# Holding seven V heads on chip instead of four, with FFN weights in four column blocks, in a decode attention layer with its backward pass

## The chip, the cores and the metric

One core of one Trainium2 chip. Times are device microseconds of a whole execution; a trace covers one profiled execution and its span is about 2 us shorter than the time. The kernel before was run again beside each experiment, on the same chip: its single runs lie between 814.0 and 827.2 us over all chips, so each experiment is compared with the runs of before that it shared. The changed kernel was not run again beside the experiments: where a text below says "less than the changed kernel", the two medians come from different rounds, and as the medians of before differ by up to 3.7 us between rounds, such a difference is good to some 4 us.

Ratios are computed as the mean time of one kernel's runs over the mean of the other's in the same rounds, so they are not quite the ratios of the medians quoted.

## The reference

One token goes through a pre-layernorm attention block and a bilinear FFN block; the outputs are the result and the gradients of all inputs.

```python
# x: 1 x 448; 16 query heads, 8 KV heads of 256; caches 8 x 32768 x 256, the window is the last W = 4096 rows
q = layernorm(x) @ wq
p = softmax(q @ K[window].T / 16);  o = p @ V[window]
h  = x + o @ wo
h2 = h + (g * u) @ w_down        # g = layernorm(h) @ w_gate, u = layernorm(h) @ w_up, F = 1792
# returned: h2, dx, dK_cache, dV_cache, dwq, dwo, dw_gate, dw_up, dw_down
```

What matters here: dK_cache and dV_cache have the shape of the caches, 134 MB each. Outside the window they are zero, so 235 MB of zeros must be stored. Inside the window each KV head needs its K and V in a forward pass (pass 1), and its V once more in the backward pass (pass 2), which writes 2 MB of dV and 2 MB of dK per head.

## The kernel before

GpSimd issues 103 zero stores of 2 MB from one zero buffer. They wait for nothing but room in their queue. SP issues everything else.

```python
zeros = ar(0, ZW)                       # ZW = 8192 elements, 16 KB per partition
for g in range(G):
    for o in (out_2, out_3):            # dK, dV
        if g == G - 1 and o is out_3:
            continue
        reg = zero_rows(o, g, 0, 5 if g == G - 1 else NZ, ZW)
        for i in range(reg.shape[0]):
            ZQ.dma_start(out=reg[i], in_=zeros)          # ZQ = nc.gpsimd
```

Pass 1 has three K slots and four V slots (HELD = 4). V of the heads 0 to 3 is overwritten by V of the heads 4 to 7; those four stay for pass 2, which starts with them and loads the others again.

```python
for g in range(G):
    p_f = p_next
    if g + 1 < G:
        p_next = scores(g + 1)          # transposes of K, q.K, softmax
    moments(g, p_f)                     # M = V.T (p*K), and p.V, p.K
    if g + 3 < G:
        load_kv(K_slot[g % 3], A_k_cache, g + 3)
    if g + HELD < G:
        load_kv(V_slot[g % HELD], A_v_cache, g + HELD)
    if g == G - 2:
        LD.dma_start(out=wo_sb, ...)    # LD = nc.sync (SP)
# ... the whole of w_gate and w_up, in rows of 10752 bytes per partition; w_down was loaded in pass 1
```

In the middle stand the out projection, the FFN forward and backward, and the gradient of o. Pass 2:

```python
stage = [...] * 3                        # three buffers of 2 MB for dV and dK
order = list(range(HELD, G)) + list(range(HELD))
for it, g in enumerate(order):
    ... dots(V_sb, ...)                  # transposes of V, do.V
    stV, stK = stage[stc % 3], stage[(stc + 1) % 3]
    stc += 2
    for l in range(8):                   # 16 rank-4 products, copied from PSUM into stV and stK
        ...
    for o_ap, st_ in ((out_3, stV), (out_2, stK)):
        LD.dma_start(out=o_ap[0, g, Sk - W:, :]..., in_=st_)
    for job in plan[it]:                 # weight gradients: outer products, stored from two buffers
        job()
    if it == 6:
        nc.vector.memset(ar(VB, ZW), 0.0)          # a slot that is free by now
for o, g, n0, n1, f in late_jobs:        # the last nine 2 MB pieces of zeros, 18.9 MB, as four stores of 4 MB and one of 2 MB
    ... LD.dma_start(out=reg[i], in_=ar(VB + ZW - f, f))
```

The late zero stores read a slot that is cleared only near the end, so they cannot be issued earlier.

Of the kernel before, what the change touches and what calls it, by code (L numbers as in the profile page):

```python
# [21 lines left out]
NB = 7  # L22
# [5 lines left out]
HELD = 4  # L28
# [4 lines left out]
def kernel(  # L33
# [13 lines left out]
    VB = 16 * KB  # L47
    MB = VB + HELD * 16 * KB
    RB = MB + 32 * KB
    TOTAL = RB + 81 * KB + 128  # L50
    arena = const.tile([128, TOTAL], bf16)

    def ar(off, n):
        return arena[:, off:off + n]

    zeros = ar(0, ZW)
    V_slot = [ar(VB + 16 * KB * i, T * Dh).rearrange("p (t d) -> p t d", d=Dh) for i in range(HELD)]
    M_sb = [ar(MB + 4 * KB * g, 4 * KB).bitcast(f32).rearrange("p (v h d) -> p v h d", v=2, h=2) for g in range(G)]
    wqA = ar(MB, 24 * KB).rearrange("p (c j) -> p c j", c=3)
    wqB = ar(MB + 24 * KB, 4 * KB)  # L60
    K_slot = [ar(RB + o * KB, T * Dh).rearrange("p (t d) -> p t d", d=Dh) for o in (16, 32, 0)]
    KT_slot = [ar(RB + (48 + 2 * i) * KB, 2 * KB).rearrange("p (e t k) -> p e t k", t=4, e=2) for i in range(3)]
    pK_slot = [ar(RB + (54 + 4 * i) * KB, 4 * KB).rearrange("p (t h d) -> p t h d", t=4, h=2) for i in range(2)]
    wo_sb = ar(RB, 28 * KB).rearrange("p (j n) -> p j n", n=D)
    wg_sb = [ar(RB + 28 * KB + 6272 * i, 3 * F).rearrange("p (c f) -> p c f", c=3) for i in range(2)]
    wgB_sb = [ar(RB + 28 * KB + 6272 * i + 3 * F, FH) for i in range(2)]
    junk = ar(RB + 105 * KB // 2, F)
    o_rows = junk[0:H, 0:2 * Dh].bitcast(f32)
    om = junk[:, 2 * Dh:4 * Dh].bitcast(f32).rearrange("p (a j) -> p a j", a=8)
    h_row = ar(RB + 119 * KB // 2, 2 * D)[0:1].bitcast(f32)  # L70
    diag = ar(RB + 56 * KB, F)
    wd_sb = ar(RB + 62 * KB, 2 * NB * D).rearrange("p (h b n) -> p h b n", h=2, b=NB)
    dg_bc = ar(RB + 62 * KB + 6272, 2 * F).rearrange("p (i f) -> p i f", i=2)
    junk0 = ar(RB + 62 * KB + 6272, D)
    ppad = [ar(RB + 62 * KB + 6272 + 512 * (i + 1), T * H).rearrange("p (t h) -> p t h", h=H) for i in range(2)]
    rows1, rows2 = [ar(o, 2 * KB)[0:16].bitcast(f32) for o in (RB + 62 * KB + 6272 + 1536, RB + 70 * KB)]
    ok_rows = ar(RB + 62 * KB + 6272 + 2560, 2 * KB)[0:H].bitcast(f32).rearrange("p (k d) -> p k d", k=2)
    stage = [ar(RB + 16 * KB * i, T * Dh).rearrange("p (t d) -> p t d", d=Dh) for i in range(3)]
    Rbig = [ar(o, 8 * KB).rearrange("p (l n) -> p l n", l=8) for o in (RB + 48 * KB, MB + 24 * KB)]
    VT_slot = [ar(RB + (56 + 2 * i) * KB, 2 * KB).rearrange("p (e t k) -> p e t k", t=4, e=2) for i in range(3)]  # L80
    dq_bc = ar(RB + 62 * KB, H * Dh)
    Zr = ar(RB + 72 * KB, KB).rearrange("p (w k i) -> p w k i", w=4, k=32)
    wst = [ar(MB + 12 * KB * i, 12 * KB) for i in range(2)]
    wq2A = ar(VB + 2 * 16 * KB, 24 * KB).rearrange("p (c j) -> p c j", c=3)
    wq2B = ar(VB + 2 * 16 * KB + 24 * KB, 4 * KB)
# [16 lines left out]
    ones_bf = const.tile([128, 128], bf16)  # L102
    nc.vector.memset(ones_bf[:], 1.0)
    ones_f = const.tile([128, 128], f32)
    nc.vector.memset(ones_f[:], 1.0)
# [7 lines left out]
    late_jobs = [(out_2, G - 1, 5, 7, 2 * ZW), (out_3, G - 1, 0, 6, 2 * ZW), (out_3, G - 1, 6, 7, ZW)]  # L113
# [24 lines left out]
    E_f = const.tile([H, 128], f32)  # L138
    E_ps = ps_t.tile([H, 128], f32, tag="tmp")
    nc.tensor.transpose(E_ps[:], ET_f[:], ident_f[:])  # L140
    nc.vector.tensor_copy(out=E_f[:], in_=E_ps[:])


    def to_columns(row, dt, out_ps, name):
        dup = small.tile([1, 128], dt, tag="dup" + name, bufs=1)
        nc.vector.tensor_copy(out=dup[:].rearrange("o (m w) -> o m w", w=2), in_=row[:, 384:D].unsqueeze(2).to_broadcast([1, 64, 2]))
        one = ones_bf if dt == bf16 else ones_f
        for c in range(3):
            nc.tensor.matmul(out_ps[:, c:c + 1], lhsT=row[:, c:384:3], rhs=one[0:1, 0:1], start=True, stop=True)
        nc.tensor.matmul(out_ps[:, 3:4], lhsT=dup[:], rhs=one[0:1, 0:1], start=True, stop=True)  # L150

    def layernorm(row, dt, name):
# [6 lines left out]
        ps = ps_t.tile([128, 6], f32, tag="tmp")  # L159
        to_columns(row, dt, ps, name)  # L160
        nc.tensor.matmul(ps[:, 4:6], lhsT=ones_f[0:1, 0:128], rhs=mv[:, 0:2], start=True, stop=True)
        xc = const.tile([128, 6], f32, tag=name + "xc")
        nc.vector.tensor_copy(out=xc[:], in_=ps[:])
        xT = const.tile([128, 4], f32, tag=name + "xT")
        nc.vector.tensor_scalar(out=xT[:], in0=xc[:, 0:4], scalar1=xc[:, 4:5], scalar2=xc[:, 5:6], op0=ALU.subtract, op1=ALU.mult)
        X_b = const.tile([128, 5], bf16, tag=name + "Xb")
        nc.vector.tensor_copy(out=X_b[:, 0:3], in_=xT[:, 0:3])
        nc.vector.tensor_scalar(out=X_b[:, 3:5], in0=par_f[:], scalar1=xT[:, 3:4], scalar2=None, op0=ALU.mult)
        return xc[:, 5:6], xT, X_b

    def layernorm_bwd(dcat, xT, rstd, plus, name):
# [3 lines left out]
        nc.tensor.matmul(ps[:].rearrange("p a b -> p (a b)"), lhsT=ones_f[:], rhs=dcat[:], start=True, stop=True)  # L175
# [14 lines left out]
    load_kv(K_slot[0], A_k_cache, 0)  # L190
    load_kv(V_slot[0], A_v_cache, 0)
    load_kv(K_slot[1], A_k_cache, 1)
    load_kv(V_slot[1], A_v_cache, 1)
    LD.dma_start(out=wd_sb, in_=B_w_down.rearrange("(h p b) n -> p h b n", h=2, b=NB))
    load_kv(K_slot[2], A_k_cache, 2)
    load_kv(V_slot[2], A_v_cache, 2)
    load_kv(V_slot[3], A_v_cache, 3)
# [16 lines left out]

    d_hh = const.tile([128, 2, NB], f32)
    for h in range(2):
        for b in range(NB):
            nc.vector.tensor_tensor_reduce(out=junk0, in0=wd_sb[:, h, b, :], in1=dh2_bc[:], scale=1.0, scalar=0.0,
                                           op0=ALU.mult, op1=ALU.add, accum_out=d_hh[:, h, b:b + 1])
# [33 lines left out]
    with tc.tile_pool(name="ps_m", bufs=1, space=bass.MemoryType.PSUM) as ps_m, \  # L253
            tc.tile_pool(name="ps_x", bufs=1, space=bass.MemoryType.PSUM) as ps_x, \
# [3 lines left out]
        def scores(g):  # L258
            fill_vpad(g % 2, qT_bf[:, 4 * g:4 * g + 4].rearrange("p (k e) -> p e k", e=2))
            sT_ps = dots(K_slot[g % 3], KT_slot, vpad[g % 2], rows1, ps_c, "cols", lambda q, XT, ps: nc.scalar.copy(out=XT, in_=ps))  # L260
# [8 lines left out]
            nc.tensor.matmul(nb_ps[:], lhsT=ones_f[0:1, 0:128], rhs=gmax[:], start=True, stop=True)  # L269
# [8 lines left out]
            nc.tensor.matmul(tot_ps[:], lhsT=ones_f[:, :], rhs=psums[:], start=True, stop=True)  # L278
# [11 lines left out]
        def moments(g, p_f):  # L290
            K_sb, V_sb = K_slot[g % 3], V_slot[g % HELD]
            M_ps = ps_m.tile([128, 2, 2 * Dh], f32, tag="M")
            for c in range(8):
# [5 lines left out]
                for i in range(4):  # L299
                    t = 4 * c + i  # L300
                    for vh in range(2):
                        nc.tensor.matmul(M_ps[:, vh, :], lhsT=V_sb[:, t, vh * 128:(vh + 1) * 128], rhs=pK[:, i, :, :].rearrange("p h d -> p (h d)"),  # L302
                                         start=(t == 0), stop=(t == T - 1))
            for k, X_sb in enumerate((V_sb, K_sb)):
                for t in range(T):
                    nc.tensor.matmul(ok_ps[:, k, :], lhsT=ppad[g % 2][:, 8 * (t % 4) + t // 4, :], rhs=X_sb[:, t, :],  # L306
                                     start=(g == 0 and k == 0 and t == 0), stop=(g == G - 1 and k == 1 and t == T - 1))
            for vh in range(2):
                nc.scalar.copy(out=M_sb[g][:, vh].rearrange("p h d -> p (h d)"), in_=M_ps[:, vh, :])  # L309
# [3 lines left out]
        for g in range(G):  # L313
# [4 lines left out]
            if g + 3 < G:  # L318
                load_kv(K_slot[g % 3], A_k_cache, g + 3)
            if g + HELD < G:  # L320
                load_kv(V_slot[g % HELD], A_v_cache, g + HELD)
            if g == G - 2:
                LD.dma_start(out=wo_sb, in_=A_wo.rearrange("(p j) n -> p j n", j=32))
        nc.vector.tensor_copy(out=ok_rows, in_=ok_ps[:])

    for i, w in enumerate((B_w_gate, B_w_up)):
        LD.dma_start(out=wg_sb[i], in_=w[0:384, :].rearrange("(p c) f -> p c f", c=3))
        LD.dma_start(out=wgB_sb[i], in_=w[384:D, :].rearrange("r (h f) -> (r h) f", h=2))

    with tc.tile_pool(name="ps_mid", bufs=3, space=bass.MemoryType.PSUM) as ps_mid, \  # L330
            tc.tile_pool(name="workm", bufs=1) as workm:
        okT_ps = ps_mid.tile([128, 2, 2, H], f32, tag="mid")
        for k in range(2):
            for dh in range(2):
                nc.tensor.transpose(okT_ps[:, k, dh, :], ok_rows[:, k, dh * 128:(dh + 1) * 128], ident_f[0:H, 0:H])
        ob_ps = ps_mid.tile([128, 8, 32], f32, tag="mid")
        nc.tensor.matmul(ob_ps[:].rearrange("p a j -> p (a j)"), lhsT=E_f[:], rhs=ok_rows[:, 0, :], start=True, stop=True)
# [13 lines left out]
        gu_ps = ps_mid.tile([128, 2, 2, NB], f32, tag="mid")  # L351
        for i in range(2):
            for b in range(NB):
                nc.tensor.matmul(gu_ps[:, i, :, b], lhsT=wgB_sb[i][:, b::NB], rhs=X2_b[:, 3:5], start=True, stop=False)
# [288 lines left out]
```

## Time and profile before

| | before |
|---|---|
| median of the first runs | 821.52 us (821.11 to 824.68, 3 runs) |
| bytes moved | 339.0 MB, 216 MB of them GpSimd's zeros |
| TensorE, VectorE busy | 55%, 45% |
| DMA engines busy | 90% or more in 38 of 40 slices |

The page of the kernel before. The span is cut into 40 slices; "DMA" is the busy share of the 16 DMA engines in tenths (9 means 90% or more), GB/s is what they moved. q0 is GpSimd's queue, q1 is SP's.

```profile
span 819.2 us, 8365 instructions
DMA  8999999999999999999999999999999999999991
GB/s 332 429 427 434 430 426 431 429 429 426 431 428 426 431 413 423 430 429 430 420 425 422 412 428 419 414 426 417 429 413 428 430 430 427 427 424 436 422 413 59
q0 software_dynamic: 14832, 216.01, 62.3%
q1 hardware_dynamic: 9494, 122.48, 35.4%
```

DMA is full from start to end, at about 427 GB/s. The Trainium skill ("DMA: Bandwidth & Descriptors", Specifications) gives 435 GB/s as the ceiling of the on-chip side, and the trace agrees within 2%. Nothing else is near full. So the time is bytes over bandwidth, as long as some DMA is always ready to run.

That something is always ready is due to the zeros. The next lines are groups and timeline lines of before: the last matmuls of pass 1 (L306), the first of the dq product that opens pass 2 (L453), the last zero store of GpSimd, the first and last store of a head. In the group lines the three times are the least, median and greatest duration in ns, and then the first and last start in us; in the timeline, start and duration in us.

```profile
L306 PE MATMUL ok_ps<-arena x512: 272/273/421, 57.6 to 308.0; 128*16 128x256 bf16 x171
L453 PE MATMUL dqb_ps<-arena,doT_f x64: 379/379/796, 392.4 to 415.1; 128*128 128x256 f32 x64
...
725.09 0.53 POOL L120 DMA_DIRECT2D out_dram<-arena  x1 [11.21 <-DMA out_dram<-arena]
...
466.79 1.61 SPq L584 DMA_DIRECT2D out_dram<-arena  x2
...
758.88 1.62 SPq L584 DMA_DIRECT2D out_dram<-arena  x2
```

This gives four stretches: pass 1 to 308 us, the middle to 392, then 75 us to the first head's store, then pass 2. The table of windows puts the engines beside them (busy us of each engine, granted clock, share of the DMA engines, GB/s):

```profile
0.00:308.00 308.00, 261.81 (x1858) 141.49 (x1859) 137.97 (x656) 79.54 (x116) 30.02 (x57) 0.96 1.00 422
308.00:392.00 84.00, 32.40 (x230) 18.57 (x228) 51.74 (x134) 5.17 (x10) 8.35 (x16) 0.60 1.01 427
392.00:467.00 75.00, 54.50 (x334) 35.97 (x333) 34.75 (x89) 21.65 (x33) 6.46 (x12) 0.78 1.01 419
467.00:819.00 352.00, 103.76 (x736) 46.88 (x733) 141.83 (x276) 86.22 (x142) 15.19 (x29) 0.60 0.95 403
```

In the middle TensorE works 32 of 84 us, waiting for loads and for VectorE, and the DMA share is still 1: the zeros fill it. In the kernel before the zeros last: GpSimd issues its last store at 725 us, and the late zeros on SP cover the rest.

### The profile page before, as it was taken

Reading aid. Unit: us, or ns where it says so; the run is one execution under the profiler, and the core shown is the slowest. Engines: PE = TensorE matmul, PEld = TensorE weight load, DVE = VectorE, ACT = ScalarE, POOL = GpSimd, SP = SyncE. Lnnn points to the kernel's source line nnn. Section 1 sums busy time; section 2 is a strip of 40 time slices with the busy share of each in tenths; the row PEclk is TensorE's granted clock in tenths of the full one; section 3 lists DMA queues with packets and bytes.
Section 4 is the critical chain, followed back from the end, with each engine's and each line's share of the span. In section 5 each row is a group of like instructions: output and inputs, shape, how many; then the busy total and the mean of one; then the engine's idle time right before and its main releaser. Section 6 shows DMA issues by size and latency. Waiting matters only on the chain.

```text
span 819.2 us, 8365 instructions
## 1 busy us (share of the span) xinstructions
PE 452.5 (55%) x3151; PEld 242.9 (30%) x3151; DVE 366.3 (45%) x1153; ACT 192.6 (24%) x301; POOL 60.0 (7%) x112
## 2 busy tenths in 40 slices
PE   0566999999999997510937817352430437111000
PEld 0332545545545554210833413220210213000000
DVE  3023762562652652489234927354455447334000
ACT  0232134134043110200112606141230235123000
POOL 4000000000001100111110000000000000000000
PEclk9967999999999997565876967755655577555555
DMA  8999999999999999999999999999999999999991
GB/s 332 429 427 434 430 426 431 429 429 426 431 428 426 431 413 423 430 429 430 420 425 422 412 428 419 414 426 417 429 413 428 430 430 427 427 424 436 422 413 59
DMA packets 24366, 339.01 MB, mean 414 GB/s; under 512 B 2691, under 2 KB 3334, under 8 KB 4358
## 3 DMA queue, kind: packets, MB, share of 16 engines
q0 software_dynamic: 14832, 216.01, 62.3%
q1 hardware_dynamic: 9494, 122.48, 35.4%
q8 instruction: 24, 0.39, 0.2%
q14 instruction: 16, 0.13, 0.0%
HBM read 57.89 MB, written 280.59 MB: 413 GB/s over the span
## 4 chain that ended last, share of the span: by engine, by line
DMA 28%; DVE 10%; PE 8%; ACT 2%; issue 1%; another core or an unknown queue 1%; SPq 0%; DVEq 0%; ACTq 0%
DMA out_dram<-arena 28%; DVE arena L412 2%; PE rows_ps L246 2%; PE d_ps L574 2%; DVE arena L581 2%; DVE arena L582 2%; PE tr_ps L243 1%; PE dqb_ps L453 1%; DVE arena L467 1%; ACT arena L579 1%; ACT arena L534 1%; DVE arena L387 0%; DVE arena L566 0%; DVE arena L536 0%
## 5 line engine op out<-in xcount | busy, mean ns | idle before, releaser
L298 DVE TENSOR_SCALAR arena<-arena,p_f 128x256 bf16<-128x256 bf16 x512 | 109.3, 280 | 63.0 <-PE M_ps L302 63.0
L574 PE MATMUL d_ps<-arena,rT 32*128 32x512 bf16 x256 | 41.5, 520 | 163.5 <-ACT arena L579 117.3
L302 PE MATMUL M_ps<-arena 128*128 128x512 bf16 x512 | 124.3, 384 | 0.0
L243 PE MATMUL tr_ps<-ident_bf,arena 128*128 128x128 bf16 x1024 | 88.2, 237 | 34.7 <-DVE arena L536 14.4
L120 POOL DMA_DIRECT2D out_dram<-arena x103 | 55.4, 539 | 665.0 <-DMA out_dram<-arena 665.0
L246 PE MATMUL rows_ps<-arena,vpad 128*16 128x512 bf16 x256 | 86.7, 438 | 24.8 <-DVE arena L536 16.4
L243 PEld LDWEIGHTS <-arena 128*128 128x128 bf16 x1024 | 66.3, 106 | 71.3 <-issue 58.9
L260 ACT COPY arena<-tr_ps 128x1024 bf16<-128x1024 bf16 x64 | 61.7, 1015 | 99.0 <-PE tr_ps L243 99.0
L582 DVE CAST arena<-d_ps 128x512 bf16<-128x512 f32 x64 | 43.6, 681 | 84.7 <-DMA out_dram<-arena 84.7
L574 PEld LDWEIGHTS <-rT 32*128 32x128 bf16 x256 | 10.5, 96 | 186.1 <-issue 145.9
L579 ACT CAST arena<-d_ps 128x512 bf16<-128x512 f32 x64 | 38.0, 594 | 108.6 <-DMA out_dram<-arena 108.6
L302 PEld LDWEIGHTS <-arena 128*128 128x128 bf16 x512 | 46.4, 99 | 51.3 <-issue 7.4
L306 PE MATMUL ok_ps<-arena 128*16 128x256 bf16 x512 | 58.7, 274 | 0.9 <-DVE arena L287 0.9
L578 ACT CAST arena<-d_ps 128x512 bf16<-128x512 f32 x64 | 37.6, 588 | 69.9 <-PE d_ps L574 69.8
L581 DVE CAST arena<-d_ps 128x512 bf16<-128x512 f32 x64 | 43.9, 686 | 21.4 <-PE d_ps L574 21.0
L306 PEld LDWEIGHTS <-arena 128*16 128x16 bf16 x512 | 45.2, 90 | 15.6 <-issue 5.1
L534 ACT COPY arena<-tr_ps 128x1024 bf16<-128x1024 bf16 x32 | 32.5, 1015 | 54.3 <-PE tr_ps L243 49.7
L246 PEld LDWEIGHTS <-vpad 128*16 128x16 bf16 x256 | 19.6, 91 | 72.8 <-issue 63.9
L309 ACT COPY arena<-M_ps 128x512 f32<-128x512 f32 x16 | 8.6, 589 | 80.0 <-PE M_ps L302 80.0
L536 DVE COPY arena<-tr_ps 128x1024 bf16<-128x1024 bf16 x32 | 21.8, 683 | 3.6 <-PE tr_ps L243 3.6
L467 DVE TENSOR_SCALAR arena<-arena,xT 128x1792 bf16<-128x1792 bf16 (+1 forms) x9 | 8.0, 893 | 33.1 <-DMA out_dram<-arena 21.5
L412 DVE CUSTOM_DVE_ANT_0 arena<-arena,dh_bc 128x448 bf16<-128x448 bf16 x32 | 20.0, 624 | 1.1
(184 smaller groups left out, 339.0 us busy)
## 6 DMA issues: line engine op xcount, KB each, us to landing
out_dram<-arena POOLq DMA_DIRECT2D x103, 2048.0 KB, 59.9
out_dram<-arena SPq DMA_DIRECT2D x17, 2048.0 KB, 27.5
arena<-in_A_v_cache_dram SPq DMA_DIRECT2D x12, 2048.0 KB, 39.2
arena<-in_A_k_cache_dram SPq DMA_DIRECT2D x8, 2048.0 KB, 21.3
out_dram<-arena SPq DMA_DIRECT2D x4, 4096.0 KB, 42.5
arena<-in_A_wq_dram SPq DMA_DIRECT2D x2, 3072.0 KB
arena<-in_A_wo_dram SPq DMA_DIRECT2D x1, 3584.0 KB
out_dram<-arena SPq DMA_DIRECT2D x3, 1024.0 KB, 44.1
```

The source lines that it names most:

```text
L120: ZQ.dma_start(out=reg[i], in_=zeros)
L243: nc.tensor.transpose(tr_ps[:, dh, i, :], X_sb[:, 4 * q + i, dh * 128:(dh + 1) * 128], ident_bf[:])
L246: nc.tensor.matmul(rows_ps[:], lhsT=pad[:, dh, 16 * q:16 * q + 16], rhs=XT[:, dh].rearrange("p t k -> p (t k)"), start=(q == 0 and dh == 0 ...
L260: sT_ps = dots(K_slot[g % 3], KT_slot, vpad[g % 2], rows1, ps_c, "cols", lambda q, XT, ps: nc.scalar.copy(out=XT, in_=ps))
L298: nc.vector.tensor_scalar(out=pK[:, i, hh, :], in0=K_sb[:, t, :], scalar1=p_f[:, 8 * i + c, hh:hh + 1], scalar2=None, op0=ALU.mult)
L302: nc.tensor.matmul(M_ps[:, vh, :], lhsT=V_sb[:, t, vh * 128:(vh + 1) * 128], rhs=pK[:, i, :, :].rearrange("p h d -> p (h d)"), start=(t == ...
L306: nc.tensor.matmul(ok_ps[:, k, :], lhsT=ppad[g % 2][:, 8 * (t % 4) + t // 4, :], rhs=X_sb[:, t, :], start=(g == 0 and k == 0 and t == 0), ...
L534: nc.scalar.copy(out=XT, in_=ps)
L574: nc.tensor.matmul(d_ps[:, qi].rearrange("p w d -> p (w d)"), lhsT=rT[32 * q:32 * (q + 1), :], rhs=RB_[32 * q:32 * (q + 1), l, :], start=T ...
L579: nc.scalar.copy(out=stK[:, t:t + 2, :], in_=d_ps[:, :, 1, :])
L581: nc.vector.tensor_copy(out=stV[:, t:t + 2, :], in_=d_ps[:, :, 0, :])
L582: nc.vector.tensor_copy(out=stK[:, t:t + 2, :], in_=d_ps[:, :, 1, :])
```

## The change

The intent: three loads of V fewer in pass 2 (9 instead of 12), 6.3 MB. Seven V slots take the room of the K slots, the FFN weights and the third stage buffer, so all of these are laid out anew (the removed lines on slots and stage are shortened, "..." stands for lines left out):

```diff
-HELD = 4
+FB = ((0, 4), (512, 4), (1024, 4), (1536, 2))          # FFN columns in four blocks
-V_slot, K_slot: 4 and 3 slots of 16 KB per partition
+S = [16 * KB * (i + 1) for i in range(7)]
+V_at = [seq(o) for o in (S[5], S[0], S[1], S[2], S[3], S[4], S[6], S[5])]
+K_at = [seq(o) for o in (RB, S[6], S[4], S[5], RB, S[6], S[5], RB)]
-stage = three slots
+stage = [seq(MB), seq(MB + 16 * KB), seq(S[6])]
...
+def load_ffn(f0, nw):
+    n = 128 * nw
+    LD.dma_start(out=wd_b[:, 0:nw, :], in_=B_w_down[f0:f0 + n, :].rearrange("(p w) n -> p w n", w=nw))
+    for i, w in enumerate((B_w_gate, B_w_up)):
+        LD.dma_start(out=w_b[i][:, 0:3 * n].rearrange("p (c f) -> p c f", c=3), in_=w[0:384, f0:f0 + n].rearrange("(p c) f -> p c f", c=3))
+        LD.dma_start(out=wB_b[i][:, 0:n], in_=w[384:D, f0:f0 + n])
...
+            elif g == 5:
+                load_kv(V_at[6], A_v_cache, 6)
+            elif g == 6:
+                load_kv(V_at[7], A_v_cache, 7)
+                load_wo(27, 32)
+        load_wo(0, 19)
+        load_ffn(*FB[0])
...
+        for q, (f0, nw) in enumerate(FB):
+            if q:
+                load_ffn(f0, nw)                         # into the same buffers
+            ... forward, gradient and reductions of this block
...
-        order = list(range(HELD, G)) + list(range(HELD))
+        order = [1, 2, 3, 4, 5, 6, 7, 0]
-            stV, stK = stage[stc % 3], stage[(stc + 1) % 3]
+            stV, stK = stage[stc % 2], stage[(stc + 1) % 2]
+            if it >= 6:
+                stV, stK = stage[(stc - 12) % 3], stage[(stc - 11) % 3]
...
-            if it == 6:
-                nc.vector.memset(ar(VB, ZW), 0.0)
-                LD.dma_start(out=reg[i], in_=ar(VB + ZW - f, f))
+                LD.dma_start(out=reg[i], in_=zeros)      # late zeros: now from the first zero buffer
```

The last line looks like tidying. It takes the wait away from the late zero stores, and the scheduler moves them: in the order of SP's instructions all nine now stand in pass 1, three before the load of K5, four before V5, two before K6. (They are also cut from five stores into nine of 2 MB.)

## The prediction

> **What bounds the kernel now.** The DMA engines. The page's slices show them at 90% or more in all but the first and last of 40 slices, about 427 GB/s; TensorE is busy 55%. 339.0 MB move, 216 MB of them zeros stored by the GpSimd queue, which keeps eight 2 MB stores in flight. That stream fills every gap: pass 1 is TensorE-bound (31.3 us per head, last moments evacuated at 301 us), the middle ends near 392 us (first dq matmul), pass 2 stores from 467 to 800 us, and the engines never idle. GpSimd issues its last zero store at 725 us (its timeline).
>
> **Intended gain.** V is loaded 9 times instead of 12: 6.3 MB less, 14.7 us at 427 GB/s. If the engines stayed full: about 807 us. I expect they don't.
>
> **What the change adds** (order of instructions, buffer map).
> 1. The nine "late" zero stores no longer wait for a cleared buffer, so they are scheduled on the SP queue among the loads of pass 1, before K5, V5 and K6. SP gets half the engines beside the zeros, so each costs the loads behind it 9.8 us. V6 and V7 also have just one buffer, free only one head before use. A replay of the queues with these times ends pass 1 near 355 us (before: about 308).
> 2. FFN weights come in four blocks through one set of buffers, each waiting for the block before. Gate and up rows become 1024-byte runs: 64 packets per engine and block. In the trace each SP packet waits for one 16 KB zero packet (0.61 us), whatever its own size: a 224 KB load of 1792-byte rows took 11.0 us to land, a 2 MB K load at best 14.9. The Trainium skill (DMA: Bandwidth & Descriptors, "Queues, rings and completion order") says the engines take queues in turn at packet granularity; the trace agrees, about 25 packets of each per us. So a block takes 43 us to load and 60 us per cycle; the last part of wo queues behind block 0. Before, this stretch took some 45 us. The middle ends near 650 us instead of 392.
> 3. Pass 2 has two stage buffers for six of eight heads instead of three. By my replay the zeros run out near 665 us, before the first head's store (about 715 us); then nothing fills the DMA. A head costs 14 us to fill (744.9 to 758.8 in before) plus about 16 us for its stores to land alone (4.4 us to start, 16 packets of 0.61, receipt), plus job work: 32 us. Seven more heads and the last landing: 240 us.
>
> **Critical path.** The saved 15 us count only while DMA is full; the added waits (some 260 us) hide only while zeros last, and they don't.
>
> **Predicted time:** 945 us, 885 to 995 (8 in 10). Chances: faster by over 2%: 0.02; within 2%: 0.06; slower by over 2%: 0.92.
>
> **What would show it.** Total about 332.7 MB; DMA full to 640-690 us, then slices at 30-60%; end of moments to first dq matmul 250-320 us, FFN matmuls waiting 30-45 us per block for gate and up; transposes stalled for K6, moments for V6 and V7; gate and up loads of 384 KB taking 15-25 us each; GpSimd's last zero store near 605 us; pass 2 waiting for its stores with only the SP queue active.
>
> **What would make it wrong.** If small packets of one DMA were taken several at a time, the middle would shrink by 100 us or more and zeros would last longer: about 860 us. If pass 2 overlapped better than one head per 32 us, I am 20-50 us too high. If the engines stay full, 807 us.

## The result, and the profile after

The changed kernel took 887.98 us (887.25 to 888.48, 4 runs) against 821.32 us for before: ratio 1.083, 95% interval 1.077 to 1.089. Slower, inside the predicted range, near its low end.

The page of the changed kernel:

```profile
span 886.2 us, 8621 instructions
DMA  8999999999999999999999999999999198354444
GB/s 339 430 431 429 429 430 426 433 427 427 419 430 429 416 424 429 425 428 427 428 427 428 428 428 429 428 427 425 422 417 387 56 412 324 132 238 189 189 190 190
q0 software_dynamic: 14832, 216.01, 57.5%
q1 hardware_dynamic: 13750, 116.19, 31.6%
```

The bytes fell as intended, 122.5 to 116.2 MB on SP. DMA is full to about 680 us, then uneven, and moves 189 to 238 GB/s over the last five slices. The marks of the four stretches, as for before (L331 ends pass 1, L501 opens pass 2, L131 is a zero store, L638 a head's stores):

```profile
L331 PE MATMUL ok_ps<-arena x512: 272/273/382, 57.4 to 364.7; 128*16 128x256 bf16 x171
L501 PE MATMUL dqb_ps<-arena,doT_f x64: 379/379/797, 607.4 to 629.8; 128*128 128x256 f32 x64
...
636.37 0.53 POOL L131 DMA_DIRECT2D out_dram<-arena  x1 [4.54 <-DMA out_dram<-arena]
...
665.63 2.29 SPq L638 DMA_DIRECT2D out_dram<-arena  x2
...
828.36 46.55 SPq L638 DMA_DIRECT2D out_dram<-arena  x6
```

And the table of windows of the changed kernel:

```profile
0.00:365.00 365.00, 264.89 (x1859) 143.64 (x1859) 130.00 (x629) 77.41 (x112) 32.10 (x60) 0.90 1.00 422
365.00:607.00 242.00, 40.15 (x242) 22.50 (x241) 62.36 (x234) 8.90 (x22) 24.44 (x46) 0.53 1.01 428
607.00:666.00 59.00, 54.48 (x402) 37.62 (x402) 30.95 (x76) 28.70 (x53) 3.19 (x6) 0.96 1.01 420
666.00:886.00 220.00, 99.25 (x692) 44.39 (x691) 147.50 (x305) 83.66 (x139) 0.00 (x0) 0.64 0.55 230
```

| stretch | before, us | after, us | DMA share before | after |
|---|---|---|---|---|
| pass 1 | 308 | 365 | 1.00 | 1.00 |
| middle | 84 | 242 | 1.01 | 1.01 |
| to the first head store | 75 | 59 | 1.01 | 1.01 |
| pass 2 | 352 | 220 | 0.95 | 0.55 |

The account closes, within the rounding of the shares. In pass 2 the DMA engines now idle for 220 x 0.45 = 99 us, before for 352 x 0.05 = 18 us: 81 us more idle time. Less the 14.7 us of saved bytes (6.3 MB at 427 GB/s), that makes some 67 us, and the spans differ by 67.0.

Note that TensorE works about as much in the middle as before (40 against 32 us): nearly all of the 158 us that were added there are waiting. The waits in the changed kernel (who waited, at what line, for what: us in total, times, longest):

```profile
PEld L413 <- DMA arena<-in_B_w_gate_dram: 71.3, 3, 24.8
PE tr_ps L264 <- DMA arena<-in_A_k_cache_dram: 49.7, 3, 38.6
PE ao_ps L390 <- DMA arena<-in_A_wo_dram: 44.2, 1, 44.2
PE gu_ps L413 <- DMA arena<-in_B_w_up_dram: 40.2, 3, 13.6
PE M_ps L327 <- DMA arena<-in_A_v_cache_dram: 22.3, 2, 16.3
```

All five are waits for SP loads. The 38.6 us one is K6, which stands behind the nine zero stores on SP. The V waits are V7 (16.3 us, nothing to do meanwhile) and V6. The 44.2 us one is the last part of wo, queued behind the 64 packets per engine of the first FFN block. The rest, the gate and up weights, comes once per further block. One block on TensorE's timeline; the bracket is the idle time before and what ended it:

```profile
453.81 0.26 PE L413 MATMUL gu_ps<-X_b,arena 128*128 128x1 bf16 x3 [24.46 <-DMA arena<-in_B_w_gate_dram]
456.85 0.19 PE L414 MATMUL gu_ps<-X_b,arena 64*128 64x1 bf16 x1 [2.78 <-DMA arena<-in_B_w_gate_dram]
...
471.31 0.23 PE L413 MATMUL gu_ps<-X_b,arena 128*128 128x1 bf16 x3 [13.31 <-DMA arena<-in_B_w_up_dram]
474.45 0.19 PE L414 MATMUL gu_ps<-X_b,arena 64*128 64x1 bf16 x1 [2.90 <-DMA arena<-in_B_w_up_dram]
```

Some 43 us of waiting for 1.4 MB (with w_down), which at 427 GB/s are 3 us of work. The reason is in the packets. Started packets per microsecond in that stretch, counted in the trace by queue and size (the clock of the packets starts some 10.5 us before the span's):

```
us     GpSimd, 16384 B   SP, 1024 B
449.0        24              30
450.0        25              26
451.0        23              27
452.0        25              26
453.0        25              29
```

About one SP packet per zero packet, whatever their sizes. Equal counts would also fit turns of several packets each, but the times of the records settle it. Of the zero packets that start between 440 and 450 us of the span, 90% start within 8 ns of the end of an SP packet (of random moments, 15% do), and 81% of the SP packets start within 8 ns of the end of a zero packet: a turn is one packet. The records give 611 ns to a 16384-byte packet and 46 ns to a 1024-byte one, so SP gets 7% of the engines' time here. The Trainium skill ("DMA: Bandwidth & Descriptors", "Queues, rings and completion order") says that each engine goes round the queues that have work, at packet granularity, which the trace shows. The same page ("Issuing engines are not separate DMA queues") says that transfers interleave on the same 16 engines whoever issues them; here that interleaving sets the pace of the FFN blocks (e2 and e5 below).

### The profile page after: what moved, and what is told of

The parts are those of the page before. It is cut to its first block, busy times and chain, and to the rows that moved or that the text cites. A ratio compares the mean times of both kernels' runs of the same rounds, so it can differ in the third digit from the quotient of the medians.

```text
span 886.2 us, 8621 instructions
## 1 busy us (share of the span) xinstructions
PE 458.8 (52%) x3193; PEld 248.1 (28%) x3193; DVE 370.8 (42%) x1243; ACT 198.7 (22%) x325; POOL 59.7 (7%) x112
## 2 busy tenths in 40 slices
DMA packets 28624, 332.75 MB, mean 375 GB/s; under 512 B 2979, under 2 KB 7206, under 8 KB 8742
## 4 chain that ended last, share of the span: by engine, by line
PE 38%; DMA 34%; DVE 16%; another core or an unknown queue 4%; ACT 4%; issue 1%; SPq 1%; DVEq 0%; ACTq 0%
DMA arena<-in_B_w_up_dram 13%; PE M_ps L327 12%; PE ok_ps L331 6%; DMA out_dram<-arena 6%; PE rows_ps L267 6%; DMA arena<-in_A_k_cache_dram 5%; DMA arena<-in_A_wo_dram 5%; PE tr_ps L264 4%; DMA arena<-in_A_v_cache_dram 4%; DVE arena L636 3%; DVE arena L635 3%; PE d_ps L628 2%; DVE arena L458 2%; ACT arena L282 2%; PE dqb_ps L501 2%
## 5 line engine op out<-in xcount | busy, mean ns | idle before, releaser
L264 PE MATMUL tr_ps<-ident_bf,arena 128*128 128x128 bf16 x1024 | 88.2, 237 | 75.2 <-DMA arena<-in_A_k_cache_dram 49.7
L264 PEld LDWEIGHTS <-arena 128*128 128x128 bf16 x1024 | 67.3, 106 | 119.6 <-DMA arena<-in_A_k_cache_dram 50.2
L267 PE MATMUL rows_ps<-arena,vpad 128*16 128x512 bf16 x256 | 84.4, 429 | 31.0 <-DVE arena L590 15.0
L131 POOL DMA_DIRECT2D out_dram<-arena x103 | 55.1, 536 | 576.6 <-DMA out_dram<-arena 576.6
L327 PEld LDWEIGHTS <-arena 128*128 128x128 bf16 x512 | 47.0, 100 | 75.6 <-DMA arena<-in_A_v_cache_dram 22.7
L413 PE MATMUL gu_ps<-X_b,arena 128*128 128x1 bf16 x84 | 7.2, 177 | 111.5 <-DMA arena<-in_B_w_gate_dram 70.4
L331 PE MATMUL ok_ps<-arena 128*16 128x256 bf16 x512 | 57.5, 273 | 0.9 <-DVE arena L309 0.9
L331 PEld LDWEIGHTS <-arena 128*16 128x16 bf16 x512 | 45.4, 90 | 13.9 <-issue 3.4
L188 ACT CAST arena<-bc_ps 128x256 bf16<-128x256 f32 (+1 forms) x32 | 11.1, 347 | 156.3 <-PE bc_ps L187 155.1
L413 PEld LDWEIGHTS <-arena 128*128 128x128 bf16 x84 | 5.0, 119 | 112.9 <-DMA arena<-in_B_w_gate_dram 71.3
```

The costliest lines, as they stand in the source:

```text
L264: nc.tensor.transpose(tr_ps[:, dh, i, :], X_sb[:, 4 * q + i, dh * 128:(dh + 1) * 128], ident_bf[:])
L267: nc.tensor.matmul(rows_ps[:], lhsT=pad[:, dh, 16 * q:16 * q + 16], rhs=XT[:, dh].rearrange("p t k -> p (t k)"), start=(q == 0 and dh == 0 ...
L327: nc.tensor.matmul(M_ps[vh][:], lhsT=V_sb[:, t, vh * 128:(vh + 1) * 128], rhs=pK[:, i, :, :].rearrange("p h d -> p (h d)"), start=(t == 0) ...
L331: nc.tensor.matmul(ok_ps[:, k, :], lhsT=ppad[g % 2][:, 8 * (t % 4) + t // 4, :], rhs=X_sb[:, t, :], start=(g == 0 and k == 0 and t == 0), ...
```

## The experiments

**e1: late zeros back at the end.** In the changed kernel, the slot of V7 is cleared after its last use and is the source of the nine late stores.

```diff
             if it == 6:
+                nc.vector.memset(ar(S[5], ZW), 0.0)
...
-                LD.dma_start(out=reg[i], in_=zeros)
+                LD.dma_start(out=reg[i], in_=ar(S[5], ZW))
```

> The changed kernel, with the nine 2 MB zero stores of the SP queue made to wait for a cleared slot near the end (their source is the slot of V7, cleared after its last use), as in the kernel before. My theory (added waits use up the zero stream): the 38.6 us wait for K6 in pass 1 goes, the end of pass 1 and the first head store come 30 to 40 us earlier (about 630 instead of 666), the GpSimd zeros also end earlier (about 636), and the total falls to 850-865 us. Rival (moving these stores early is harmless, the loss is all in the middle and pass 2): 880 or more.

Measured: 843.72 us (2 runs), ratio to before 1.032 (1.022 to 1.043). That is 44 us less than the changed kernel, and below the expected range. The first head's stores were issued at 630.93 us, as expected, and the last zero store of GpSimd at 586.74 (about 636 expected); the wait for K loads fell from 49.7 to 11.5 us. The rival falls. Two effects come together: pass 1 no longer stalls, and 18.9 MB (44 us at full rate) are left to fill the end. The timelines show where the time fell: the first head's stores came 35 us earlier (630.93 against 665.63), and the rest, 8 us, is in pass 2 (from these stores to the end of the span 213 us against 221).

**e2: zero packets of 4 KB.** The same zeros, read from the first 4 KB of the buffer four times over, so that each packet is a quarter as long.

```diff
-                ZQ.dma_start(out=reg[i], in_=zeros)
+                ZQ.dma_start(out=reg[i].rearrange("p (a f) -> p a f", f=2048), in_=zeros[:, 0:2048].unsqueeze(1).to_broadcast([128, ZW // 2048, 2048]))
```

> The changed kernel, with the zero stores of the GpSimd queue cut into packets of 4 KB instead of 16 KB; bytes and data the same. My theory (each SP packet waits for one zero packet): a block of 64 small packets loads in about 14 us instead of 43, the cycle of a block falls from about 51 us to about 25, K6 no longer stalls, the first head store comes near 520 instead of 666 us, DMA is full nearly to the end, and the total falls to 820-840 us although 4 KB packets move zeros some 4% slower. Rival (the blocks are slow because they are serial, or because 1 KB rows are slow in themselves): cycle of a block stays at 45-50 us, total 880-910.

Measured: 822.82 us (2 runs), ratio 1.007 (0.997 to 1.016), 65 us less than the changed kernel. The first head's stores came at 500.33 us (about 520 expected), and the wait for K fell from 49.7 to 3.1 us. SP's loads were not touched, yet their blocks came at twice the pace. The first load of each block (w_down, L237) in the changed kernel:

```profile
427.91 0.33 SPq L237 DMA_DIRECT2D arena<-in_B_w_down_dram  x1
...
478.95 0.33 SPq L237 DMA_DIRECT2D arena<-in_B_w_down_dram  x1
...
528.21 0.34 SPq L237 DMA_DIRECT2D arena<-in_B_w_down_dram  x1
```

and with the short zero packets:

```profile
339.27 0.34 SPq L237 DMA_DIRECT2D arena<-in_B_w_down_dram  x1
...
363.88 0.34 SPq L237 DMA_DIRECT2D arena<-in_B_w_down_dram  x1
...
387.18 0.34 SPq L237 DMA_DIRECT2D arena<-in_B_w_down_dram  x1
```

The cycle fell from 51.0 and 49.3 us to 24.6 and 23.3. The blocks are still in series and the rows still 1024 bytes; only the neighbour in the other queue changed. The rival falls. DMA was full in all slices but the first and last in this run, and the time is then bytes over a slightly lower bandwidth: a 4096-byte packet took 159 ns, four of them 636 against 611 for 16 KB.

**e3: three stage buffers again.** Head 6 goes first in pass 2, and its V slot becomes the third stage buffer.

```diff
-        order = [1, 2, 3, 4, 5, 6, 7, 0]
+        order = [6, 2, 3, 1, 4, 5, 7, 0]
...
-            stV, stK = stage[stc % 2], stage[(stc + 1) % 2]
-            if it >= 6:
-                stV, stK = stage[(stc - 12) % 3], stage[(stc - 11) % 3]
+            stV, stK = stage[stc % 3], stage[(stc + 1) % 3]
```

(V0 is loaded again after the fourth head instead of the first, wq after the sixth instead of the fifth.)

> The changed kernel with head 6 first in pass 2, so that its V slot is a third stage buffer from the second head on, as in the kernel before (V0 and wq are loaded again three and one heads later). My theory: after the zeros end, a head costs fill plus store with two buffers (30 us); with three the store is partly hidden, 23-26 us per head, total 850-865. If pass 2 is bound by TensorE or VectorE work and not by its buffers: 880-890.

Measured: 859.15 us (2 runs), ratio 1.051 (1.041 to 1.061), 29 us less than the changed kernel. From the first head's stores (667.95 us) to the seventh's (826.15) it is 26.4 us per head; in the changed kernel the stores of the first six heads stand at 665.63, 706.44, 735.37, 773.62, 803.11 and 828.36 us, 32.5 us per head. Pass 2 was bound by its buffers, as expected, and still is to some extent.

**b1: late zeros early, in the kernel before.** One part of the change alone.

```diff
-                LD.dma_start(out=reg[i], in_=ar(VB + ZW - f, f))
+                LD.dma_start(out=reg[i], in_=zeros)
```

> The kernel before, with only its late zero stores freed from their wait (source is the zero buffer that is ready from the start, 2 MB each as in the changed kernel). My theory: its loads have slack (two loads of 9.8 us per 31.3 us head) and its zeros still outlast the rest, so DMA stays full and the total stays within 812-835 us. Rival (this reordering alone makes the change slower): 855 or more.

Measured: 817.77 us (2 runs) beside 817.83, ratio 1.001 (0.992 to 1.010). Transposes now waited 48.1 us for K, and the first head's stores came at 504.50 us instead of 466.79. The end did not move. The same edit that costs the changed kernel 44 us costs this one nothing: its zeros last long enough to hide the stall (GpSimd issued its last one at 753 us).

**e5: half the packets (wrong result).** Each block of w_gate and w_up is read as one run of 3072 bytes per partition, so the values are wrong; bytes, loads, waits and series are the same.

```diff
-            LD.dma_start(out=w_b[i][:, 0:3 * n].rearrange("p (c f) -> p c f", c=3), in_=w[0:384, f0:f0 + n].rearrange("(p c) f -> p c f", c=3))
+            LD.dma_start(out=w_b[i][:, 0:3 * n], in_=w[0:384, :].rearrange("(p c) f -> p (c f)", c=3)[:, f0:f0 + 3 * n])
```

> Wrong result on purpose: the changed kernel, with the gate and up blocks read as one run of 3072 bytes per partition instead of three of 1024. Bytes, number of loads, waits and block structure stay; packets per engine and block fall from 64 to 32. My theory (the number of packets times one zero packet sets the load): a block loads in about 23 us instead of 42, its cycle falls from about 50 us to about 30, the first head store comes 70 to 85 us earlier (about 585 instead of 666), total 835-860. Rival (blocks are slow because they are in series, whatever their packets): cycle 45 us or more, total 875 or more.

Measured: 860.47 us (2 runs), ratio 1.051 (1.046 to 1.057), just above what was expected. Blocks started at 414.46, 447.62 and 480.63 us, a cycle of 33 us instead of 50; the first head's stores came at 600.97. With e2 this shows both factors: the time of a block goes with the number of its packets and with the length of a zero packet.

**c1: e1 and zero packets of 8 KB together.** The cut is that of e2 with 4096 elements instead of 2048.

> The changed kernel with two repairs: late zeros at the end (as e1) and zero stores of the GpSimd queue in packets of 8 KB. 8 KB packets move 1% slower (309 ns against 611 for 16 KB). Theory: cycle of a block about 35 us, first head store near 560, DMA full to within 30 us of the end, total 810-826, so about level with the kernel before or 1% better.

Measured: 811.38 us (2 runs), ratio 0.991 (0.986 to 0.997). Blocks started at 355.46, 388.63 and 420.28 us, the first head's stores at 540.13.

**c2: c1 and e3 together.**

> As c1, and with head 6 first in pass 2 so that three stage buffers serve from the second head on. Theory: DMA full to the end, the time is bytes over bandwidth: 332.7 MB, 14.7 us less than before, plus some 5 us for the 8 KB packets: 0.985 to 1.0 of the kernel before. If the third buffer still matters beside c1, c2 is faster than c1 by over 5 us; if DMA is already full in c1, they are equal within 3 us.

Measured: 802.28 us (801.69 to 802.89, 4 runs), ratio 0.980 (0.976 to 0.984): about 2% less than the kernel before, more than expected, and 9 us less than c1 on the same chip. That it is faster is clear of noise; whether by 2%, the interval leaves open. Its page:

```profile
span 799.9 us, 8595 instructions
DMA  8999999999999999999999999999999999999888
GB/s 330 430 428 430 423 427 425 423 422 417 419 426 415 419 418 422 423 427 421 425 422 423 424 425 419 416 418 421 397 422 428 425 403 425 432 426 430 372 367 373
```

Where the third buffer matters beside the other two repairs is the end: c1 moved 273 and 207 GB/s in its last two slices, c2 367 and 373.

**c3: short zero packets only during the FFN blocks.** As c2, but zero stores 50 to 79 have packets of 4 KB and the others 16 KB.

```diff
+                f = 2048 if 50 <= zn < 80 else ZW
+                zn += 1
```

> As c2, but only the 30 zero stores that run during the FFN blocks (numbers 50 to 79) are cut, into packets of 4 KB, and the others keep 16 KB. Theory: cycle of a block about 25 us, less loss of bandwidth overall (4% of 30 stores, some 6 us) and the shortest middle: 0.98 to 0.995 of the kernel before. If 16 KB packets in pass 2 starve the head stores again, it is slower than c2.

Measured: 815.41 us (814.0 to 816.26, 4 runs), ratio 0.996 (0.992 to 1.000), 13 us slower than c2 on the same chip. The first head's stores came even a little earlier (538.31 against 543.11 us), but the second to fifth heads then took 36.6, 49.8, 56.2 and 41.2 us each, against 30.1, 36.8, 39.5 and 44.0 in c2. My main expectation missed; its last sentence held. Beside 16 KB packets the head stores (16 KB packets too) get half of the packet time, beside 8 KB packets two thirds (51% in c3 from 545 to 557 us, 66% in c2 from 550 to 562), and the heads of pass 2 wait for these stores. In pass 2 the two runs differ in the zero packets alone, which points to this share as the cause; the first heads' stores came at nearly the same time in both.

**c4: all zeros on GpSimd's queue.** As c2, with the nine late stores appended to GpSimd's 103.

> As c2, but the nine late zero stores are appended to the GpSimd queue (8 KB packets) instead of standing on the SP queue among the head stores. Theory: a filler that never stands in front of a head store leaves fewer gaps in the last 60 us (c2 has 370 GB/s in its last three slices): 0.97 to 0.98 of the kernel before, up to 8 us less than c2. Rival (bandwidth is already spent, the order of the end does not matter): equal to c2 within 3 us.

Measured: 803.45 us (802.98 to 804.80, 6 runs), ratio 0.979 (0.976 to 0.983). Its ratio and that of c2 are equal within their intervals (they ran on different chips): here the rival was right. DMA was full up to the last slice (229 GB/s in that one), so there was little left to fill.

**b2: 8 KB zero packets in the kernel before.**

> The kernel before with only its GpSimd zero stores cut into 8 KB packets. Theory: DMA is full there anyway, so shorter waits of its loads buy nothing and the 1% slower packets cost up to 5 us: 1.00 to 1.01 of the kernel before, though its pass 2 starts earlier. Rival (the cut is a gain by itself and explains c2 without the change): 0.985 or less.

Measured: 820.05 us (4 runs), ratio 0.999 (0.994 to 1.004). The stores of its first and last head:

```profile
429.13 0.93 SPq L584 DMA_DIRECT2D out_dram<-arena  x2
...
650.83 1.62 SPq L584 DMA_DIRECT2D out_dram<-arena  x2
```

Against 466.79 and 758.88 us in before: the last head's stores are issued 108 us earlier, and the total is the same. So the kernel before is bound by bytes, and the 2% of c2 and c4 is not due to the shorter packets by themselves.

## Why the prediction was right, and where its sizes were off

The direction, the three causes and the main effect were right: the filler runs out early in pass 2, and from then on DMA idles. Point by point:

- **Saved bytes:** 332.75 MB moved, 332.7 predicted. Worth 15 us only with DMA full: c2 and c4 save 16 to 17 us, the changed kernel none.
- **Late zeros on SP stall K6, and V6 and V7 come late:** 38.6 us for K6, 16.3 us for V7. Pass 1 ended at 365 us (355 predicted). e1 shows the price of the moved zeros, 44 us; b1 shows that it is no price of that edit alone. V6 and V7 were not tested by themselves.
- **Packet by packet:** confirmed by e2 and e5. The matmuls of a block waited some 43 us (30 to 45 predicted). A gate load landed after a median of 23.4 us, but an up load after 38.1, because it queues behind the gate load; I had said 15 to 25 for both.
- **Filler ends:** DMA was full to about 680 us (640 to 690 predicted). GpSimd's last store was issued at 636 us, not near 605.
- **Two stage buffers:** e3 recovers 29 us.

What was mis-sized: the terms of the text add up to 715 + 240 = 955 us, already rounded down to 945; the span is 886. Three terms were too long, by 43, 7 and 20 us.

1. **"60 us per cycle", "the middle ends near 650 us"**: it ended at 607, although pass 1 ended 10 us later than predicted. The middle took 242 us instead of 295. The cycles were 51.0, 49.3 and about 47 us. The load term (43 us) was about right: 46.5 us from the w_down load (427.91) to the last release of the up matmuls (474.45). The serial work after the last landing was not: from the last gate and up matmul (475.40 us) to the next w_down load (478.95) it took 3.6 us. That accounts for some 32 of the 53 us. The rest cannot be placed: the prediction gives no figure for the stretch from wo's landing to the end of block 0, which took 17 us (410.88 to 427.91).
2. **First head's store:** 58 us after the first dq matmul, where I had 65. With point 1 it was issued at 666 us instead of 715. The zeros did run out when I had said (their packets thin out at about 670 us; 665 predicted), so what did not come is the stretch of 50 us between the two in which nothing fills the DMA; it idles only from about 685.
3. **"A head costs 32 us", 240 us from the first store to the end:** 220 us. The intervals between the heads' stores were 40.8, 28.9, 38.3, 29.5, 25.3, 25.3 and 20.4 us. That the first five average 32.5 is luck, as two terms were off in opposite directions. Alone, a head's two stores landed 11 us after their issue (828.36 to 839.61), not 16: their first packet started after 0.8 us, not 4.4. (Beside the zeros of before, the store issued at 347.77 did take 4.3 us to start.) With 14 us to fill, that makes the two intervals of 25.3, which hold no other large transfer. The four before them hold weight-gradient stores and took 4 to 16 us more; I had 2 for that. Only the last head uses the third buffer (the code still gives the seventh the first two).

The condition that I named for being wrong, small packets taken several at a time, did not hold: the packets alternate one to one. The second, that pass 2 might beat a head per 32 us, held in part: these are the 20 us of point 3.

Still open: what the changed kernel would take with the late zeros kept for the end but pass 1 still stalled, that is, what each effect of e1 is worth alone. c2 and c4 gain 16 to 17 us where the saved bytes are worth 14.7; the interval of c2 (13 to 19 us) covers that, so there is no difference to explain.

## What to carry to other kernels

In these runs a background stream that fills the DMA engines made waits elsewhere free, but only until it ran out: before lengthening a serial stretch, compare what is left of the filler with the work that must still follow. When two DMA queues share the engines packet by packet, as here, a load made of many short rows pays one packet of the other queue for each of its own; cut the background's packets, or read longer rows, and the urgent queue gets its share back. Taking away a wait can move an instruction: look at the new order before calling an edit neutral.

## What the Trainium skill lacked or had wrong

- "DMA: Bandwidth & Descriptors", "Queues, rings and completion order": it says an engine drains a packet of typically 9 to 17 descriptors before it turns to the next queue. Here the turn was one contiguous run: 23 to 25 packets of 16384 bytes and 26 to 30 of 1024 bytes started per us, and 90% of the former began where one of the latter ended. It draws no consequence for a kernel: 1.4 MB, mostly in rows of 1024 bytes, took some 43 us beside 16 KB zero stores, and a cut of the zero stores alone to 4 KB took the cycle of such a block from 50 to 24 us.
- The same page, "Rules for kernel authors": no rule says to give a background stream short packets. 8 KB cost little per byte (309 ns against 611 for 16 KB, so 1%), and with the other two repairs they are part of the step from 888 to 802 us.
